# A planned attention and GeGLU block on one core: x1's statistics move from ScalarE to VectorE, the ones columns of V are set in four pieces, and the planner paces more zero fills

## The chip, the cores and the metric

The kernel runs on 1 core of one Trainium2 chip. The metric is device microseconds of one execution. A second, profiled execution gives the trace that is read here; its own time is given beside its span.

## The reference

One pre-norm transformer block without a mask, S = 2048 rows, D = 512, 32 heads of 16, F = 1792, all tensors bfloat16:

```python
x  = A_x                                             # (1, 2048, 512)
q, k, v = split_heads(layernorm(x) @ A_wqkv)         # 32 heads of 16
p  = softmax((q @ k.T) * 16 ** -0.5)                 # 2048 x 2048 for each head
h  = x + merge_heads(p @ v) @ A_wo
h2 = h + (gelu(layernorm(h) @ B_w_gate) * (layernorm(h) @ B_w_up)) @ B_w_down
```

`layernorm` is (x - mean) / sqrt(var + 1e-5) without weights, `gelu` is the tanh form.

## The kernel before

**Who decides the order.** The kernel is written as streams of operations (`Op`, one engine each, with a duration that the author expects). `Sched.run` plays these streams against its own clock when the kernel is built, picks the operation that can start first, breaks near ties by priority (`prio`, plus a random part of up to 0.3 from `self.rng`), and so writes one fixed instruction list for each engine. On the chip every engine works through its list in order and waits only for semaphores of what it reads or overwrites. A `gate` (such as `C["exp"] >= 1`) and an expected duration (such as the megabytes of a load) shape the list and leave no wait on the chip. Every change of a number in the planner therefore can move instructions anywhere in the kernel.

**The start.** x comes as 16 tiles of 128 rows in chunks of four: x0 in two loads, x1, x2, x3 in one load each, between them the pieces of the weights (`loads`). `ln1(c)` makes the statistics of a chunk: VectorE's `bn_stats` and `bn_aggr`; `ln1_rstd` makes 1/sqrt(var + eps) on GpSimd (a power); `ln1_norm` writes the normalised tile, on VectorE for chunks 0 and 1, on GpSimd for chunks 2 and 3. `ln1_T` turns the tile: for chunks 0 and 1 by four TensorE transposes and a copy from PSUM (ScalarE for tile 1, VectorE for the others, lines L1452 and L1454), for chunks 2 and 3 by a DMA transpose on SyncE's queue (L1437). Tile 4, the first of x1, has its statistics from ScalarE (lines L1388 and L1390: a sum and a sum of squares, then five small GpSimd operations, L1392 to L1400). `first()` projects K and Q of the first four heads tile by tile; `proj_kq` and `proj_v` do the rest, by need. `ones_v` sets the ones column behind every head of V (L1369), with which the product P·V also gives the softmax's denominator. `warm()` keeps TensorE busy with matmuls of no use until the first scores.

**The long middle.** A step of scores (`qk`) writes two PSUM banks, and ScalarE takes one `exp` of 128x1024 from them (`exps`, L1335). There are two pairs of banks, so the scores of a step wait for the exp two steps earlier. A part of the score tiles (124 groups of four) goes to VectorE instead, which makes their exponentials by integer arithmetic (`dconv` L1705, `dchain` L1718 to L1725, one of the four multiplications on GpSimd). `pv` and `group_pv` multiply by V. Query rows are done in chunks of 512, 512, 256, 256, 256, 128 and 128 (`CHUNKS`); while the next chunk's exps run, `post`, `gates`, `gelu`, `ups` and `downs` of the chunk before are woven in. A chunk's gelu is two ScalarE instructions (one for 128 rows) between two loads of ScalarE's function table (L1984 and back to exp at L1335). The last chunk's gelu goes straight from PSUM (L1967), after the exps have ended.

**Zero fills.** `fill()` lets the planner insert a matmul of zeros (L2051) when TensorE has done less than `RATE` columns per us over its last work. The debt `owed` grows with `RATE`; a fill goes into a gap of 0.217 us or more at a debt of 100, into a smaller gap at 300, into none at 800 (`OWED`). A fill is not inserted where, by the planner's clock, it would delay the scores that are due.

```python
if n < OWED[0] or (gap < TMM and n < OWED[1]) or (gap < 0.06 and n < OWED[2]):
    return False
```

Of the kernel before, what the change touches and what calls it, by code (L numbers as in the profile page):

```python
# [169 lines left out]
S, D, H, DH, F = 2048, 512, 32, 16, 1792  # L170
# [5 lines left out]
S, D, H, DH, F = 2048, 512, 32, 16, 1792  # L176
# [712 lines left out]
class Sched:  # L889
# [5 lines left out]
    def __init__(self, P, banks):  # L895
        self.P = P
        self.t = {n: 0.0 for n in P.ENGINES}
        self.done = {}
        self.streams = []
        self.banks = [(0.0, b) for b in banks]  # L900
        self.now = 0.0
        self.fill = None
        self.debt = (0.0, 0.0)
        self.pipe = 0.0
        self.lent = set()
        self.rng = random.Random(11)
        self.early = True
        self.wake = None
        self.port = 0.0
        self.room = lambda: False  # L910
        self.mode = "f"
        self.rows = [0.0] * 4
        self.due = self.INF
# [224 lines left out]
DB = 1  # L1138
HB = 0
CHP = -2.1  # L1140
RATE = 950
OWED = (100, 300, 800)
CHUNKS = (512, 512, 256, 256, 256, 128, 128)
F16, U16 = mybir.dt.float16, mybir.dt.uint16
# [60 lines left out]
def fast_path(nc, P, base0, ARENA, pbank, flag, A_x, A_wqkv, A_wo, B_x, B_w_gate, B_w_up, B_w_down, out):  # L1205
# [17 lines left out]
    VA = VF[:, 0:NVA].rearrange("p (t h i) -> p t h i", h=H, i=17)  # L1223
# [7 lines left out]
    x_sb = at("x_sb", [128, NT, D], BF16)  # L1231
# [106 lines left out]
    def loads():  # L1338
        def d(o, i, key, writes, mb):
            return Op("sp", mb, lambda e: e.dma_start(out=o, in_=i), writes=writes, dma=key)  # L1340
        def w(key, a, b, mb):
            return d(wqkv_sb[:, :, a:b], wv[:, :, a:b], key, [key], mb)
        def xl(c):
            return d(x_sb[:, 4 * c:4 * c + 4, :], xv[:, 4 * c:4 * c + 4, :], ("x", c), [("x", c)], 0.5)
        yield d(x_sb[:, 0:2, :], xv[:, 0:2, :], ("x", 0, 0), [("x", 0, 0)], 0.25)
        yield d(x_sb[:, 2:4, :], xv[:, 2:4, :], ("x", 0, 1), [("x", 0, 1)], 0.25)
        yield w("wk0", 512, 640, 0.18)
        yield w("wq0", 0, 128, 0.18)
        yield xl(1)
        yield w("wB", 640, 1536, 0.95)  # L1350
        yield xl(2)
        yield w("wA", 128, 512, 0.42)
        yield xl(3)
        yield d(wo_sb[:], A_wo.rearrange("(c p) j -> p c j", p=128), "wo", ["wo"], 0.5)
# [11 lines left out]
        yield Op("pool", 0.3, lambda e: e.tensor_copy(out=ident32[:], in_=ident[:]), reads=["ident"], writes=["ident32"])  # L1366

    def ones_v():
        yield Op("pool", 2.3, lambda e: e.memset(VA[:, :, :, 16:17], 1.0), writes=["VA_ones"], gate=lambda: ("xnT", 3) in C)  # L1369
        yield Op("pool", 0.1, lambda e: e.memset(VF[:, NVA:NVA + 15], 0.0), writes=["VA_ones"])  # L1370

    def masks():
# [8 lines left out]

    def ln1(c):
        ts_ = range(4 * c, 4 * c + 4)
        sa = ts_[0:1] if c == 1 else ()
        if sa:
            sl = slice(sa[0], sa[-1] + 1)
            for t in sa:
                yield Op("act", 0.52, lambda e, t=t: e.activation(out=sqj[:], in_=x_sb[:, t, :], func=ACT.Copy, accum_out=hsum[:, t:t + 1]),  # L1388
                         reads=[xkey(c, t)], writes=["sqj", ("hsum", t)])
                yield Op("act", 0.52, lambda e, t=t: e.activation(out=sqj[:], in_=x_sb[:, t, :], func=ACT.Square, accum_out=hsq[:, t:t + 1]),  # L1390
                         reads=[xkey(c, t)], writes=["sqj", ("hsq", t)])
            yield Op("pool", 0.3, lambda e: e.tensor_scalar(out=mv[:, sl, 0], in0=hsum[:, sl], scalar1=1.0 / D, scalar2=None, op0=ALU.mult),  # L1392
                     reads=[("hsum", t) for t in sa], writes=[("mv", t) for t in sa])
            yield Op("pool", 0.2, lambda e: e.tensor_tensor(out=htmp[:, sl], in0=mv[:, sl, 0], in1=mv[:, sl, 0], op=ALU.mult),
                     reads=[("mv", t) for t in sa], writes=["htmp"])
            yield Op("pool", 0.25, lambda e: e.tensor_scalar(out=rstd[:, sl], in0=hsq[:, sl], scalar1=1.0 / D, scalar2=EPS, op0=ALU.mult, op1=ALU.add),
                     reads=[("hsq", t) for t in sa], writes=[("rstd", t) for t in sa])
            yield Op("pool", 0.2, lambda e: e.tensor_tensor(out=rstd[:, sl], in0=rstd[:, sl], in1=htmp[:, sl], op=ALU.subtract),
                     reads=[("rstd", t) for t in sa] + ["htmp"], writes=[("rstd", t) for t in sa])
            yield Op("pool", 0.75, lambda e: e.tensor_tensor(out=rstd[:, sl], in0=rstd[:, sl], in1=nhalf[:, sl], op=ALU.pow),  # L1400
                     reads=[("rstd", t) for t in sa] + ["nhalf"], writes=[("rstd", t) for t in sa])
        for t in ts_:
            if t not in sa:
                yield Op("dve", 0.605, lambda e, t=t: e.bn_stats(out=stats[:, t, :], in_=x_sb[:, t, :]), reads=[xkey(c, t)], writes=[("stats", t)])
                yield Op("dve", 0.1, lambda e, t=t: e.bn_aggr(out=mv[:, t, :], in_=stats[:, t, :]), reads=[("stats", t)], writes=[("mv", t)])
                if c == 0:
                    yield Op("dve", 0.1, lambda e, t=t: e.tensor_scalar(out=rstd[:, t:t + 1], in0=mv[:, t, 1:2], scalar1=EPS, scalar2=None, op0=ALU.add), reads=[("mv", t)], writes=[("rstd0", t)])
                sch.add(ln1_rstd(t), 2 + 7 * c if c else -7.5)
            sch.add(ln1_norm(c, t), 2 + 7 * c if c else -7.5)
# [29 lines left out]
    def ln1_T(c, t):  # L1439
        if c >= TURN_X:  # L1440
            yield turn(xnT[:, t, :, :], xn_sb[:, t % 8, :], ("xT", t % 8), [("xn", t % 8)], [("xnT", t)])
            C[("xnT", t)] = 1
            C["ln1"] += 1
            return
        b = yield Acquire(reads=[("xn", t % 8), "ident"])
        pt = pbank[:, b, :].bitcast(BF16)
        yield Op("pe", 4 * TTR, cols=512, fns=[lambda e, dc=dc: e.transpose(out=pt[:, 128 * dc:128 * dc + 128], in_=xn_sb[:, t % 8, 128 * dc:128 * dc + 128], identity=ident[:])
                             for dc in range(4)], reads=[("xn", t % 8), "ident"], writes=[("pb", b)])
        C[("xnT", t)] = 1
        o_ap, i_ap = xnT[:, t, :, :], pt[:, 0:512].rearrange("p (c s) -> p c s", c=4)  # L1450
        if t in (1,):
            yield Op("act", 0.55, lambda e: e.activation(out=o_ap, in_=i_ap, func=ACT.Copy), reads=[("pb", b)], writes=[("xnT", t)])  # L1452
        else:
            yield Op("dve", 0.333, lambda e: e.tensor_copy(out=o_ap, in_=i_ap), reads=[("pb", b)], writes=[("xnT", t)])  # L1454
        sch.release(b)
        C["ln1"] += 1
# [13 lines left out]
    def first():  # L1470

        bq, bk = {}, {}
        for t in range(4):
            hf, o = t // 2, 128 * (t % 2)
            for nm, base, bank in (("wk0", D, bk), ("wq0", 0, bq)):
                if t % 2 == 0:
                    bank[hf] = yield Acquire(reads=[nm, ("xnT", t)])
                yield Op("pe", 4 * 0.062, cols=512, fns=[MM(pbank[:, bank[hf], o:o + 128], wqkv_sb[:, dc, base:base + 128], xnT[:, t, dc, :], dc == 0, dc == 3) for dc in range(4)],
# [661 lines left out]
```

## Time and profile before

| what | value |
|---|---|
| time before, median of 4 runs | 820.89 us (819.56 to 824.0) |
| the profiled execution's own time | 819.87 us |
| its span, first to last instruction | 818.0 us |
| around the span | 1.87 us |
| mean granted TensorE clock | 0.998 |
| TensorE (PE) busy | 767.4 us, 94% of the span |
| VectorE (DVE) busy | 759.8 us, 93% |
| ScalarE (ACT) busy | 769.7 us, 94% |
| GpSimd (POOL) busy | 252.5 us, 31% |
| the 776 exps of 128x1024 on ScalarE | 722.4 us |
| zero fills (L2051) in the trace | 105 matmuls, 36.7 us (135 weight loads) |

Busy shares are means over the whole span. Matmuls are pipelined and their ends are modelled, so a TensorE that is busy 94% is not at its peak. Idle time of an engine that does not set the pace costs nothing. A few matmul records are missing from the trace: 105 fills are recorded, 135 of their weight loads.

### The profile page before, as it was taken

Reading aid. Unit: us, or ns where it says so; the run is one execution under the profiler, and the core shown is the slowest. Engines: PE = TensorE matmul, PEld = TensorE weight load, DVE = VectorE, ACT = ScalarE, POOL = GpSimd, SP = SyncE. Lnnn points to the kernel's source line nnn. Section 1 sums busy time; section 2 is a strip of 40 time slices with the busy share of each in tenths; the row PEclk is TensorE's granted clock in tenths of the full one; section 3 lists DMA queues with packets and bytes.
Section 4 is the critical chain, followed back from the end, with each engine's and each line's share of the span. In section 5 each row is a group of like instructions: output and inputs, shape, how many; then the busy total and the mean of one; then the engine's idle time right before and its main releaser. Section 6 shows DMA issues by size and latency. Waiting matters only on the chain.

```text
span 818.0 us, 20122 instructions
## 1 busy us (share of the span) xinstructions
PE 767.4 (94%) x8194; PEld 274.3 (34%) x8261; DVE 759.8 (93%) x1238; ACT 769.7 (94%) x813; POOL 252.5 (31%) x305
## 2 busy tenths in 40 slices
PE   7999999989998999999999999999998999889996
PEld 3222222222222222222233333334433443345564
DVE  7679999999999999999999999999999999999964
ACT  3899999999999999999999999999999999999981
POOL 5703345632332322122133221222222212332310
PEclk9999999999999999999999999999999999999999
DMA  6200000350011000010111100110011000010100
GB/s 206 52 8 1 7 8 7 111 186 8 14 40 33 9 8 1 8 27 20 34 28 26 27 2 20 27 28 15 7 28 28 21 8 18 19 28 15 23 15 18
DMA packets 49878, 24.33 MB, mean 30 GB/s; under 512 B 39280, under 2 KB 48752, under 8 KB 49776
## 3 DMA queue, kind: packets, MB, share of 16 engines
q1 hardware_dynamic: 49776, 22.95, 10.7%
q8 instruction: 67, 1.10, 0.6%
q14 instruction: 35, 0.29, 0.1%
HBM read 11.80 MB, written 2.10 MB: 17 GB/s over the span
## 4 chain that ended last, share of the span: by engine, by line
PE 38%; DVE 28%; ACT 18%; issue 7%; DMA 3%; POOL 1%; ACTq 0%; DVEq 0%; POOLq 0%
PE pbank L1329 25%; ACT PT L1335 15%; PE pbank L1328 12%; DVE dXE L1705 12%; DVE dXE L1720 5%; DVE dXE L1718 4%; DVE dXE L1725 3%; DMA OAT<-OA 2%; ACT GUT L1984 1%; DVE OA L1809 1%; ACT L1335 1%; DVE GUT L1999 1%; POOL dXE L1722 1%; DVE GUT L1971 1%; ACT L1984 1%
## 5 line engine op out<-in xcount | busy, mean ns | idle before, releaser
L1335 ACT ACTIVATE PT<-pbank 128x1024 bf16<-128x1024 f32 x776 | 722.4, 1075 | 14.6 <-PE pbank L1329 12.1
L1329 PE MATMUL pbank<-QT,KT 32*128 32x512 bf16 (+1 forms) x2304 | 347.9, 359 | 27.1 <-ACT PT L1335 19.0
L1705 DVE TENSOR_SCALAR dXE<-pbank 128x512 uint16<-128x512 f32 x496 | 326.0, 680 | 10.5 <-PE pbank L1329 8.7
L1722 POOL TENSOR_TENSOR dXE<-dXE 128x512 f16<-128x512 f16 x124 | 155.8, 1257 | 357.2 <-DVE dXE L1720 357.2
L1329 PEld LDWEIGHTS pbank<-QT,KT 32*128 32x128 bf16 x2304 | 91.1, 91 | 299.1 <-ACT PT L1335 208.5
L1329 PE MATMUL pbank<-PT,VA 128*32 128x256 bf16 (+2 forms) x2704 | 130.3, 292 | 0.6 <-DVE dXE L1705 0.2
L1720 DVE TENSOR_TENSOR dXE<-dXE 128x1536 f16<-128x1536 f16 x124 | 123.2, 994 | 1.2
L1725 DVE TENSOR_SCALAR dXE<-dXE 128x2048 uint16<-128x2048 uint16 x124 | 87.7, 710 | 5.2 <-POOL dXE L1722 3.6
L1718 DVE TENSOR_SCALAR dXE<-dXE 128x2048 uint16<-128x2048 uint16 x124 | 89.3, 720 | 0.1
L1329 PE MATMUL pbank<-dXE,VA 128*32 128x256 f16 (+2 forms) x1760 | 76.4, 289 | 0.7 <-DVE dXE L1725 0.5
L1328 PE MATMUL pbank<-hnT_c,wg_sb 128*128 128x256 bf16 (+2 forms) x392 | 70.3, 291 | 1.9 <-DMA hnT_c<-OnT 1.0
L1329 PEld LDWEIGHTS pbank<-PT,VA 128*32 128x32 bf16 x2704 | 47.7, 96 | 60.8 <-issue 58.5
L1831 POOL TENSOR_TENSOR Otok<-OAT,LINV 128x128 bf16<-128x128 bf16 (+2 forms) x52 | 28.3, 561 | 108.1 <-DVE LINV L1825 105.0
L1328 PE MATMUL pbank<-hnT_c,wu_sb 128*128 128x256 bf16 (+2 forms) x392 | 59.1, 289 | 2.4 <-DVE GUT L1999 1.6
L1328 PE MATMUL pbank<-wd_sb,GUT 128*128 128x512 bf16 x200 | 54.2, 381 | 3.7 <-issue 3.7
L1329 PEld LDWEIGHTS pbank<-dXE,VA 128*32 128x32 bf16 x1760 | 31.6, 96 | 30.1 <-issue 17.3
L1999 DVE TENSOR_TENSOR GUT<-pbank,GUT 128x512 bf16<-128x512 f32 (+1 forms) x57 | 36.9, 670 | 4.3 <-PE pbank L1328 3.2
L1328 PE MATMUL pbank<-xnT,wqkv_sb 128*128 128x512 bf16 (+1 forms) x152 | 38.4, 349 | 1.6 <-DMA xnT<-xn_sb 1.0
L2051 PE MATMUL pbank<-ones_bf,zero_bf 128*128 128x512 bf16 x105 | 36.7, 386 | 1.3 <-issue 1.3
L1328 PEld LDWEIGHTS pbank<-hnT_c,wu_sb 128*128 128x128 bf16 x392 | 29.8, 98 | 23.6 <-issue 9.5
L1971 DVE CAST GUT<-pbank 128x512 bf16<-128x512 f32 (+1 forms) x53 | 35.8, 675 | 2.0 <-PE pbank L1328 1.9
L1328 PEld LDWEIGHTS pbank<-hnT_c,wg_sb 128*128 128x128 bf16 x392 | 24.9, 97 | 30.9 <-issue 27.2
(89 smaller groups left out, 345.7 us busy)
## 6 DMA issues: line engine op xcount, KB each, us to landing
xres<-in_A_x_dram SPq DMA_DIRECT2D x16, 128.0 KB, 2.2
out_dram<-out_sb SPq DMA_DIRECT2D x16, 128.0 KB, 1.7
wg_sb<-in_B_w_gate_dram SPq DMA_DIRECT2D x1, 1792.0 KB, 7.2
wu_sb<-in_B_w_up_dram SPq DMA_DIRECT2D x1, 1792.0 KB, 11.2
wd_sb<-in_B_w_down_dram SPq DMA_DIRECT2D x1, 1792.0 KB, 16.3
x_sb<-in_A_x_dram SPq DMA_DIRECT2D x3, 512.0 KB, 8.3
wqkv_sb<-in_A_wqkv_dram SPq DMA_DIRECT2D x1, 896.0 KB, 7.4
x_sb<-in_A_x_dram SPq DMA_DIRECT2D x2, 256.0 KB, 3.2
```

The lines of the kernel that those rows point to most:

```text
L1328: return lambda e: e.matmul(o, l, r, start=start, stop=stop)
L1329: return lambda e: e.matmul(o, l, r, start=start, stop=stop, tile_position=tile)
L1335: return lambda e: e.activation(out=o, in_=i, func=func, **kw)
L1705: yield Op("dve", 0.603, lambda e: e.tensor_scalar(out=dXE[G["k"] % NX][:, 0, j, :], in0=pbank[:, b, :], scalar1=XMIN + 1024.0 * CENTER, s ...
L1718: yield Op("dve", 0.07 + 0.133 * n, lambda e: e.tensor_scalar(out=W, in0=X, scalar1=0x3ff, scalar2=0xb800, op0=ALU.bitwise_and, op1=ALU.bi ...
L1720: yield Op("dve", 0.066 + 0.267 * nd, lambda e: e.tensor_tensor(out=W[:, 0:nd, :].bitcast(F16), in0=W[:, 0:nd, :].bitcast(F16), in1=X[:, 0 ...
L1722: yield Op("pool", TPOOL, lambda e, j=j: e.tensor_tensor(out=W[:, j, :].bitcast(F16), in0=W[:, j, :].bitcast(F16), in1=X[:, j, :].bitcast( ...
L1725: yield Op("dve", 0.07 + 0.133 * (h1 - h0), lambda e, h0=h0, h1=h1: e.tensor_scalar(out=X[:, h0:h1, :], in0=X[:, h0:h1, :], scalar1=0x7c00 ...
L1831: yield Op("pool" if turned else "dve", 0.15 + 0.55 / len(slots) if turned else 0.06 + 0.28 / len(slots), lambda e, o4=o4, lx=lx, o_ap=o_a ...
L1971: yield Op("dve", 0.07 + 0.001042 * n * CHUNKS[c], lambda e: e.tensor_copy(out=o_ap, in_=i_ap), reads=[("pb", b)], writes=keys, extra=dE)
L1999: yield Op("dve", 0.07 + 0.001042 * n * CHUNKS[c], lambda e: e.tensor_tensor(out=o_ap, in0=u_ap, in1=o_ap, op=ALU.mult), reads=[("pb", b)] ...
L2051: return Op("pe", TMM, lambda e: e.matmul(pbank[:, b, :], zero_bf[:], ones_bf[:], start=False, stop=False, skip_group_check=True), reads=[ ...
```

## The change

Seven edits, all in the planner's input. (1) The random seed goes from 11 to 9. (2) `RATE` goes from 950 to 1000 columns per us. (3) The planner expects other sizes of four loads (wk0, wq0, x1, wB); what is loaded, and in which order, stays. (4) The ones column of V is set by four GpSimd memsets of four tiles each in place of one of sixteen, planned after the first exp and marked as users of the port that GpSimd and VectorE share. (5) Tile 4 of x has its statistics from VectorE like all others: two ScalarE passes and five small GpSimd operations go, one `bn_stats`, one `bn_aggr` and two small GpSimd operations (an add and a power) come. (6) The copies of turned tiles 0 and 2 go from VectorE to ScalarE, beside that of tile 1. (7) For tiles 2 and 3 the first projection makes Q before K.

```diff
-        self.rng = random.Random(11)
+        self.rng = random.Random(9)
...
-RATE = 950
+RATE = 1000
...
-        yield w("wk0", 512, 640, 0.18)
-        yield w("wq0", 0, 128, 0.18)
-        yield xl(1)
-        yield w("wB", 640, 1536, 0.95)
+        yield w("wk0", 512, 640, 0.3)
+        yield w("wq0", 0, 128, 0.3)
+        yield d(x_sb[:, 4:8, :], xv[:, 4:8, :], ("x", 1), [("x", 1)], 0.9)
+        yield w("wB", 640, 1536, 0.35)
...
     def ones_v():
-        yield Op("pool", 2.3, lambda e: e.memset(VA[:, :, :, 16:17], 1.0), writes=["VA_ones"], gate=lambda: ("xnT", 3) in C)
+        for q in range(4):
+            yield Op("pool", 0.6, lambda e, q=q: e.memset(VA[:, 4 * q:4 * q + 4, :, 16:17], 1.0), writes=["VA_ones"], gate=lambda: C["exp"] >= 1, port=True)
...
-        sa = ts_[0:1] if c == 1 else ()
+        sa = ts_[0:0] if c == 1 else ()
...
-        if t in (1,):
+        if t in (0, 1, 2):
             yield Op("act", 0.55, lambda e: e.activation(out=o_ap, in_=i_ap, func=ACT.Copy), reads=[("pb", b)], writes=[("xnT", t)])
...
-            for nm, base, bank in (("wk0", D, bk), ("wq0", 0, bq)):
+            for nm, base, bank in (("wk0", D, bk), ("wq0", 0, bq))[::-1 if t > 1 else 1]:
```

The instruction lists of the two built kernels differ along their whole length. In number they differ little: both have 776 exps on ScalarE and 124 groups on VectorE. Zero fills go from 135 to 203. Around the gelus ScalarE loads its function table ten times in place of twelve: the gelu of the 128-row chunk before the last, which stood one exp before the end of the exps, now stands after the last exp. Four matmuls of P·V fewer come out of the other assignment of tiles to ScalarE and VectorE.

## The prediction

> **What bounds the kernel now.** I read the page first, then ScalarE's timeline, then the timelines of GpSimd, VectorE and TensorE where ScalarE stands still. The engine table shows three engines within 10 us of each other, so shares decide nothing:
>
> ```profile
> PE 767.4 (94%) x8194; PEld 274.3 (34%) x8261; DVE 759.8 (93%) x1238; ACT 769.7 (94%) x813; POOL 252.5 (31%) x305
> ```
>
> ScalarE's timeline (start, length, engine, line, tile, then idle time before and what ended it), in the first 110 us:
>
> ```profile
> 15.42 0.47 ACT L1490 ACTIVATE QT<-pbank,qmask 128x256 bf16<-128x256 f32 x1 [4.24 <-PE pbank L1328]
> 16.61 7.44 ACT L1335 ACTIVATE PT<-pbank 128x1024 bf16<-128x1024 f32 x8 [0.71 <-PE pbank L1329]
> 27.62 7.44 ACT L1335 ACTIVATE PT<-pbank 128x1024 bf16<-128x1024 f32 x8 [3.57 <-PE pbank L1329]
> 35.43 7.55 ACT L1335 ACTIVATE PT<-pbank 128x1024 bf16<-128x1024 f32 x8 [0.38 <-PE pbank L1329]
> 44.89 41.67 ACT L1335 ACTIVATE PT<-pbank 128x1024 bf16<-128x1024 f32 x44 [1.90 <-PE pbank L1329]
> ```
>
> Eight exps for each chunk of keys, and a stall before each batch of eight, until that chunk's K is there. From exp 25 at 44.89 on ScalarE hardly stops: the windows view gives it 733.41 us of work in the 741.65 us from there to the last scores (786.54), so 8.2 us idle. I split the span at these two points: 44.9 us of start, 741.7 us in which ScalarE sets the pace, 31.5 us of end.
>
> Who sets 44.89? The chain of waits around it:
>
> ```profile
> 38.05 0.78 POOL xn_sb L1432
> 38.84 3.55 DMA xnT<-xn_sb
> 42.64 1.02 PE pbank L1328 x4
> ```
>
> GpSimd normalises tile 15 until 38.82, the tile is turned by DMA, K is projected, and 6.07 us after GpSimd's end exp 25 runs. GpSimd's timeline is without a gap from tile 8's rstd at 19.74 to there: 19.1 us for 8 tiles, 2.4 us each. So the start is GpSimd's, not that of the first exp.
>
> The first exp itself hangs on a memset. GpSimd, VectorE, TensorE in the timeline:
>
> ```profile
> 10.93 2.46 DVE L1424 TENSOR_SCALAR xn_sb<-x_sb,mv,rstd 128x512 bf16<-128x512 bf16 x1
> ...
> 10.98 2.27 POOL L1369 MEMSET VA<- 128x512 bf16 x1
> ...
> 13.45 0.40 PE L1447 MATMUL pbank<-ident,xn_sb 128*128 128x128 bf16 x4 [1.70 <-DVE xn_sb L1424]
> ```
>
> The same VectorE operation took 0.38 to 0.41 us for tiles 0 to 2; beside the memset it took 2.46, and TensorE waited for it.
>
> **The change part by part.**
>
> *Ones column in four pieces.* Same elements: 4 x 0.57 = 2.27 us on GpSimd, plus about 0.1 for each of three handoffs within the engine (0.08 to 0.1 between dependent GpSimd rows). The gate on the first exp is the planner's only: in the new list the first memset follows tile 5's power and waits for nothing. I place that by VectorE's new order (tile 5's aggregate behind tile 4's normalisation, at 12.9) at 13.9 to 16.5. Tile 3's normalisation then costs 0.4 us in place of 2.46: 2.05 off the path of the first exp. What pays is GpSimd's queue: the memsets now stand in front of the rstds of tiles 6 and 7, and all of chunks 2 and 3.
>
> A rule bears on this. *The Trainium skill, "SBUF — State Buffer", section "Who interferes with whom", says that GpSimd and VectorE's two-port modes take one shared port pair as an exclusive lock, and whoever is first keeps it for its whole instruction; by that tile 3's normalisation, first by 0.05 us in the trace, should not have waited; the first exp would then gain 0.5 in place of 2.5, and the sum, which rests on exp 25, would stay.* I go by the row, 2.46 against 0.4: starts in the trace are not grants.
>
> *Tile 4's statistics.* ScalarE loses 0.63 + 0.63 + 0.19 + 0.19 = 1.4 us (7.81 to 9.3), which held the copy of tile 1 (transposed by 8.4, copied at 9.19). VectorE gets 0.68 + 0.18, GpSimd loses five rows (0.25 + 0.19 + 0.19 + 0.19 + 0.56 = 1.38) and gets 0.22 + 0.57: 0.6 less. *Copies of tiles 0 and 2 on ScalarE*: 0.58 each where ScalarE idles, 0.42 each off VectorE. *Q before K* for two tiles: four matmuls of 0.055, about 0.2 us earlier for the last Q.
>
> *First exp.* By the new lists: wB lands at 10.9 as now, and two V matmuls that wait for it stand ahead of tile 3's transpose. Then transpose 11.4, VectorE's copy 11.8 to 12.2, Q of tile 3 from 12.45, ScalarE's Q copy 12.9, against 15.42. The exp follows 1.19 later: 14.1, 2.5 us sooner. Almost none of it survives. Ten V matmuls (2.2 us at 0.218) now stand between the scores of exp 1 and exp 2, which puts exp 2 at 16.5 to 17.5, against 17.5 now. Exp 9 needs the copies of tiles 5 to 7, which VectorE's new list puts behind four V copies (0.6 each, to 22.7); tiles 5 to 7 copied at 24.5, four K matmuls, a K copy behind four other VectorE rows to 27.3, and 0.5 to the exp: 27.8, against 27.62.
>
> *Exp 25, by GpSimd's new list.* Tile 5's rstd from 13.0 (0.94), memsets 2.65, rstds of tiles 6 and 7 1.9: 18.5. Eight tiles at 2.4, less some 0.1 where two rows in a row do not depend on each other: 37.6, against 38.82. So exp 25 comes 1.2 us sooner, at 43.7, if what follows still takes 6.07. Bounds: ScalarE itself needs from exp 17 (35.2 at best) 7.5 us for eight exps, so 42.7, a gain of 2.2; if VectorE's queue makes tile 8's statistics late by as much as GpSimd's gaps show today (1.29 us before tile 8), nothing. I take 1.2, from the row sums.
>
> *The middle.* The same exps and five chunks' gelus with their table loads stand before the last scores, so ScalarE's work there is the same 733 us. What can move is its 8.2 us of waiting, by the new seed, the other place of every piece, and 68 more fills. A fill costs TensorE 0.218 us (four 512-column matmuls start 0.87 us before what follows), 14.8 us for 68. The windows of the fills alone:
>
> ```profile
> 200.00:300.00 100.00, 13.22 (x38) 3.44 (x45) 1.00 0.09 21
> 300.00:400.00 100.00, 1.94 (x5) 0.69 (x8) 1.00 0.06 14
> ```
>
> With 45 fills (weight loads) in the first window and 8 in the second, ScalarE idled 0.23 us in the first and 0.66 in the second. Fills in gaps cost nothing. In the new list 31 of the 68 more stand ahead of score tile 600 of 2048 (at some 230 us), 7 from there to tile 1000, and 20 from tile 1000 to 1200 (some 390 to 460 us), where 26 stand today. There TensorE idles 5.0 us in the 100 us from 400 on by the windows view, about 3.5 in these 70, and 20 fills take 4.4. So the price lies between nothing and 14.8 us, nearest to the row of the first window: nothing. They also bring nothing here, as the granted clock is 1.00 in each window up to 787. *The Trainium skill, "TensorE: Matmul & The Clock Gate", section "What's actually happening", lets the clock drop only after an idle window of some 3.4 us, which speaks against more fills; by it, too, they bring nothing.* The new order by itself can take from the 8.2 us or add as much; without a row that says which, zero.
>
> *The end.* Today the exp before the last is done at 787.30, and the last waits for a gelu between two table loads:
>
> ```profile
> 787.33 1.28 ACT L1984 ACT_TABLE_LOAD   x1
> 788.62 1.70 ACT L1984 ACTIVATE GUT<-GUT 128x1792 bf16<-128x1792 bf16 x1
> 790.33 1.28 ACT L1335 ACT_TABLE_LOAD   x1
> 791.63 1.02 ACT L1335 ACTIVATE PT<-pbank 128x1024 bf16<-128x1024 f32 x1
> ```
>
> After, the last exp ends 4.3 us sooner. But TensorE was not idle meanwhile: it did 23 matmuls of the down projection (4.91 us), and from the last scores to its last matmul (812.1) it works for all but some 1.5 of 25.5 us. The new list puts behind the last scores 24 gate matmuls of 128 columns more (1.34 us), 32 of P·V more (0.7), three down matmuls fewer (0.65): 25.4 if it never waits. So the 4.3 us turn into TensorE's queue: a gain of 0.1 to 0.7, I take 0.3; 1.5 lost if the chain from last exp to last normalised tile (9.7 us) is held up.
>
> **Sum.** -1.2 (start) + 0 (middle) - 0.3 (end) = -1.5 us. The profiled execution took 819.87, so 818.4; the median stands 1.0 above it, so 819.4.
>
> **The rivals.**
>
> *A, the forecast*: ScalarE-bound as before, 1.5 us off; own range 817 to 823. For it: the exp count is the same and fills were free where they are densest.
>
> *B, the new order closes ScalarE's waits.* 14 waits for scores make 5.5 us after 50 us, the longest 0.94, at places where two-bank scores come late behind other TensorE work. If the new order halves the 8.2 us, 4.1 go, and with the start's upper end of 2.2 and the 0.3 the time is 820.89 - 6.6 = 814.3. Against it: nothing in the edits aims there.
>
> *C, the fills get onto the path (slower).* The planner's clock is not the chip's: a fill planned into a gap that is not there delays the scores by 0.218, and ScalarE with them, since two bank pairs leave one exp of slack. Half of the 68 cost 7.4: 820.9 + 7.4 - 1.5 = 826.8. It decides from 26 fills on (5.7 us, as 1.5 are gained and 4.1 are 0.5%). For it: in the 100 us from 400 on TensorE's idle time is no longer than what the new fills ask for. Against it: the first window above.
>
> *D, the edits of the start don't do what they say*: the memset meets a normalisation again (tiles 5 and 6, when they come 1.5 us sooner than I place them), or the chunk-1 copies hold exp 9 by a us or two more. Then the start gives nothing or loses 1: 820.6 to 821.6, inside A's range.
>
> **How the numbers follow.** 0.5% is 4.1 us, about what a measurement can tell from no change: faster is below 816.8, slower above 825.0. A with D has 0.46, B 0.34, C 0.20. The range runs from 813.0 (a little below B's 814.3, as its lower bound with all of the 8.2 us gone is 810) to 825.5 (C's point of decision, with most of C left out).
>
> **What would show it.** Right: first exp at 14 to 14.5; normalisations of 0.4 us and none of 2; exp 25 at 43 to 44.5; ScalarE's idle time from there to the last scores at 6 to 10 us; last exp within 2 us of the last scores, and 31 us from the last scores to the end of the span. Wrong: exp 25 not before 44.9, then GpSimd's queue was not the bound or the memsets stood in it worse than priced; ScalarE's waits for scores above 13 us, with zero fills as the instructions ahead of the late scores, is C; below 5 is B.

## The result, and the profile after

The changed kernel takes 818.6 us (median of 34 runs, 816.5 to 828.8); the kernel before took 820.9 beside it (55 runs). The ratio is 0.9973 [0.9959, 0.9987], a gain of 2.2 us: real, but within the 0.5% that were called "no change". The profiled execution took 818.25 us with a span of 816.4, against 819.87 and 818.0. The forecast was 819.4 with a sum of -1.5 us; the two profiled executions differ by 1.6. The sum fits, but by luck, not by the terms it was made of (an exp is ScalarE's 128x1024 activation; exp 25 is the first on the last quarter of the keys):

| stretch (profiled execution) | before | after | difference | forecast |
|---|---|---|---|---|
| start of span to exp 25 | 44.89 | 44.93 | +0.04 | -1.2 |
| exp 25 to last scores | 741.65 | 740.23 | -1.42 | 0 |
| last scores to end of span | 31.46 | 31.24 | -0.22 | -0.3 |

The engine table of the page, and the group of zero fills, as before with their share of records missing (203 weight loads, 163 matmuls):

```profile
PE 778.0 (95%) x8247; PEld 277.5 (34%) x8325; DVE 758.8 (93%) x1238; ACT 766.4 (94%) x809; POOL 252.2 (31%) x305
...
L2052 PE MATMUL pbank<-ones_bf,zero_bf 128*128 128x512 bf16 x163 | 55.2, 388 | 2.1 <-issue 2.1
```

**The start.** ScalarE's timeline of the changed kernel (start, length, engine, line, then idle time before and its releaser):

```profile
14.47 1.02 ACT L1335 ACTIVATE PT<-pbank 128x1024 bf16<-128x1024 f32 x1 [0.73 <-PE pbank L1329]
17.06 6.52 ACT L1335 ACTIVATE PT<-pbank 128x1024 bf16<-128x1024 f32 x7 [1.56 <-PE pbank L1329]
29.15 7.44 ACT L1335 ACTIVATE PT<-pbank 128x1024 bf16<-128x1024 f32 x8 [5.57 <-PE pbank L1329]
36.96 7.55 ACT L1335 ACTIVATE PT<-pbank 128x1024 bf16<-128x1024 f32 x8 [0.37 <-PE pbank L1329]
44.93 35.70 ACT L1335 ACTIVATE PT<-pbank 128x1024 bf16<-128x1024 f32 x38 [0.42 <-PE pbank L1329]
```

Exp 1 is 2.1 us sooner (14.47), exp 9 is 1.5 us *later* (29.15, before 27.62), and exp 25 stands where it stood. The steps before that came out as worked out: the memsets lie at 14.30 and take 2.75 us, no normalisation is held, and GpSimd ends at 37.82 (forecast 37.6, before 38.82). Tile 3's normalisation and GpSimd's memsets and last row:

```profile
9.63 0.40 DVE L1425 TENSOR_SCALAR xn_sb<-x_sb,mv,rstd 128x512 bf16<-128x512 bf16 x1
```
```profile
14.30 2.75 POOL L1370 MEMSET VA<- 128x128 bf16 x4
...
37.05 0.77 POOL L1433 TENSOR_SCALAR xn_sb<-x_sb,rstd,htmp 128x512 bf16<-128x512 bf16 x1
```

GpSimd's us was not used, because exps 9 to 24 now run back to back behind a late exp 9. The windows view shows where exp 9 is lost (the stretch and its length in us, then busy us of TensorE, weight load, VectorE, ScalarE, GpSimd; then the granted clock, DMA share and GB/s). The first two lines are of the kernel before:

```profile
20.00:22.00 2.00, 1.89 (x20) 0.69 (x20) 1.83 (x6) 2.00 (x3) 1.61 (x4) 1.00 0.00 0
22.00:24.00 2.00, 1.28 (x10) 0.48 (x10) 2.00 (x6) 2.00 (x3) 1.56 (x6) 1.00 0.27 63
```
```profile
18.00:20.00 2.00, 0.81 (x6) 0.22 (x6) 1.95 (x7) 2.00 (x4) 1.32 (x5) 1.00 0.01 4
20.00:22.00 2.00, 1.34 (x14) 0.33 (x14) 1.97 (x5) 2.00 (x3) 1.83 (x5) 1.00 0.00 0
22.00:24.00 2.00, 2.00 (x16) 1.17 (x13) 1.58 (x4) 1.58 (x2) 1.57 (x6) 0.52 0.00 0
24.00:26.00 2.00, 2.00 (x15) 0.71 (x14) 1.89 (x5) 0.00 (x0) 1.73 (x5) 0.62 0.29 66
```

The V matmuls that used to lie here are done already, so TensorE has little to do from 18 to 22 us. From 22.1 to 25.5 us, 3.4 us long, it gets half its clock, in the very stretch in which it works without a pause for tiles 5 to 7. The profiled execution of the kernel before has no such drop in its start (that of experiment 12, with the same lists up to the tail, has one at 11.3 us).

**The middle.** From exp 25 to the last scores ScalarE has the same 733 us of work and waits 7.15 us in place of 8.24; its work is 0.33 shorter (before, then after):

```profile
44.89:786.54 741.65, 704.78 (x7652) 243.74 (x7707) 714.66 (x1134) 733.41 (x771) 225.71 (x236) 1.00 0.10 25
44.93:785.16 740.23, 713.52 (x7649) 244.13 (x7718) 714.43 (x1132) 733.08 (x771) 226.00 (x236) 1.00 0.10 25
```

**The end.** The last exp is done at 786.85 (before 792.65), with no gelu ahead of it; from there to the end of the span it is 29.55 us in place of 25.35. ScalarE's last rows:

```profile
769.00 17.84 ACT L1335 ACTIVATE PT<-pbank 128x1024 bf16<-128x1024 f32 x19
786.86 1.28 ACT L2027 ACT_TABLE_LOAD   x1
788.15 0.20 ACT L2027 ACTIVATE gset<-mv 128x1 f32<-128x1 f32 x1
795.88 1.70 ACT L1985 ACTIVATE GUT<-GUT 128x1792 bf16<-128x1792 bf16 x1 [7.53 <-DVE GUT L1972]
```

### The profile page after: what moved, and what is told of

It is laid out like the page before. It is cut to its first block, busy times and chain, and to the rows that moved or that the text cites. A ratio compares the mean times of both kernels' runs of the same rounds, so it can differ in the third digit from the quotient of the medians.

```text
span 816.4 us, 20261 instructions
## 1 busy us (share of the span) xinstructions
PE 778.0 (95%) x8247; PEld 277.5 (34%) x8325; DVE 758.8 (93%) x1238; ACT 766.4 (94%) x809; POOL 252.2 (31%) x305
## 4 chain that ended last, share of the span: by engine, by line
PE 38%; DVE 35%; ACT 16%; issue 7%; DMA 2%; POOL 1%; SPq 0%; DVEq 0%; ACTq 0%; POOLq 0%
PE pbank L1329 23%; DVE dXE L1706 15%; PE pbank L1328 14%; ACT PT L1335 13%; DVE dXE L1721 6%; DVE dXE L1719 5%; DVE dXE L1726 4%; DVE GUT L1972 1%; ACT GUT L1985 1%; DMA wqkv_sb<-in_A_wqkv_dram 1%; PE pbank L2052 1%; DVE OA L1810 1%; DMA OAT<-OA 1%; ACT L1335 1%; POOL dXE L1723 1%
## 5 line engine op out<-in xcount | busy, mean ns | idle before, releaser
L1335 ACT ACTIVATE PT<-pbank 128x1024 bf16<-128x1024 f32 x776 | 722.1, 1080 | 15.6 <-PE pbank L1329 13.3
L1723 POOL TENSOR_TENSOR dXE<-dXE 128x512 f16<-128x512 f16 x124 | 157.5, 1271 | 374.4 <-DVE dXE L1721 374.4
L1329 PEld LDWEIGHTS pbank<-QT,KT 32*128 32x128 bf16 x2304 | 89.2, 91 | 290.0 <-ACT PT L1335 202.7
L1726 DVE TENSOR_SCALAR dXE<-dXE 128x2048 uint16<-128x2048 uint16 x124 | 87.8, 711 | 4.8 <-POOL dXE L1723 3.5
L1719 DVE TENSOR_SCALAR dXE<-dXE 128x2048 uint16<-128x2048 uint16 x124 | 92.0, 742 | 0.1
L2052 PE MATMUL pbank<-ones_bf,zero_bf 128*128 128x512 bf16 x163 | 55.2, 388 | 2.1 <-issue 2.1
```

Source lines behind the costliest of these rows:

```text
L1329: return lambda e: e.matmul(o, l, r, start=start, stop=stop, tile_position=tile)
L1335: return lambda e: e.activation(out=o, in_=i, func=func, **kw)
L1719: yield Op("dve", 0.07 + 0.133 * n, lambda e: e.tensor_scalar(out=W, in0=X, scalar1=0x3ff, scalar2=0xb800, op0=ALU.bitwise_and, op1=ALU.bi ...
L1723: yield Op("pool", TPOOL, lambda e, j=j: e.tensor_tensor(out=W[:, j, :].bitcast(F16), in0=W[:, j, :].bitcast(F16), in1=X[:, j, :].bitcast( ...
L1726: yield Op("dve", 0.07 + 0.133 * (h1 - h0), lambda e, h0=h0, h1=h1: e.tensor_scalar(out=X[:, h0:h1, :], in0=X[:, h0:h1, :], scalar1=0x7c00 ...
L2052: return Op("pe", TMM, lambda e: e.matmul(pbank[:, b, :], zero_bf[:], ones_bf[:], start=False, stop=False, skip_group_check=True), reads=[ ...
```

## The experiments

Ratios are to the kernel before, run beside the experiments on the same chip; in the three groups of runs its median was 821.7 (1, 2, 5, 9), 822.6 (3, 6, 10, 11) and 822.0 us (4, 7, 8, 12). Where the clock of single runs is named, it is the mean granted TensorE clock that every run has beside its time. A trace comes from one run of each, and in experiments 1, 3, 5, 6 and 12 that was the slowest of its group. The instruction lists of experiments 5 to 11 are those of the changed kernel, but for what the edit itself adds.

**1. The start's edits alone** (the changed kernel with the old seed and `RATE`).

```diff
-        self.rng = random.Random(9)
+        self.rng = random.Random(11)
-RATE = 1000
+RATE = 950
```

> The changed kernel with the old seed 11 and the old RATE 950, so the edits of the start alone. Theory 1, the edits of the start move the first exp and not exp 25, and the gain comes from the middle's new order: exp 1 at 14 to 14.5, exp 25 at 44 to 45, 820 to 821.5, no difference from before that can be told. Rival, the edits of the start carry the gain: exp 25 at 43.5 or sooner, 818 to 819.

822.1 us (12 runs), ratio 0.9998 [0.9974, 1.0023]. Here the start does all that was forecast and more: exp 1 at 13.87, exp 9 at 26.36, exp 25 at 42.53, 2.4 us sooner than before, with the clock at 1.00. Nothing of it arrives: this plan has 780 exps on ScalarE, ScalarE waits 12.7 us from exp 25 to its last exp (8.3 before), and three drops of the clock (at 200, 316 and 504 us, 20.5 us in all) lie in the profiled execution. The drops are not the whole reason: its three runs at a clock of 0.999 took 819.6, 819.6 and 820.6, no less than the kernel before at 0.998 or more (819.3, the median of 20 runs).

**2. Seed and `RATE` alone** (the kernel before with seed 9 and `RATE` 1000).

> The kernel before with seed 9 and RATE 1000 and none of the other edits. Theory 1, seed and rate carry the gain by another order of the middle: ScalarE's idle time between exp 25 and the last scores near 7 us, 818.5 to 819.5. Rival, the edits of the start carry it: 820.5 to 821.5. A third reading, the middle is a draw that each new list makes again: anywhere from 816 to 825, with ScalarE's idle time from exp 25 to the last scores moving with the time.

830.4 us (6 runs), ratio 1.0111 [1.0064, 1.0157]. 780 exps again, 12.6 us of ScalarE's waiting, exp 25 at 45.93.

**3. The changed kernel with the old seed**, `RATE` 1000.

> The changed kernel with the old seed 11 (RATE 1000 and the edits of the start stay). Its planner gives ScalarE 778 exps instead of 776 and 230 fills. Theory 1, the seed is a draw of a plan, priced by what ScalarE must do and by the clock: 2 exps more are 1.9 us, exp 25 at 42.5 as with the edits of the start alone is 2.4 us less, few clock drops: 817 to 819.5. Rival, seed 9 is what makes the kernel fast: 821 or more.

828.1 us (4 runs), ratio 1.0069 [1.0027, 1.0111]: 778 exps, 14.9 us of waiting, although exp 25 starts at 43.69. Two drops of the clock (402 and 713 us, 13.7 us in all) lie in this trace.

**4. The changed kernel with the old `RATE`**, seed 9.

> The changed kernel with RATE back at 950; seed 9 and all edits of the start stay. This is the fourth corner beside seed 11 with 950, seed 11 with 1000 and the changed kernel. The new list has 784 exps on ScalarE in place of 776. Theory that the count of exps and ScalarE's waits, both drawn anew by any number of the planner, make the time: 8 exps at 0.93 are 7.4 us on the engine that sets the pace, so 824 to 828, ratio 1.004 to 1.008, whatever the fills do. Rival, that RATE 1000 pays through its fills: the clock is lower by 0.003 to 0.01 than in the changed kernel, and the time at an equal clock is that of the changed kernel plus at most 1. Second rival, that the edits of the start are what pays: ratio 0.997 as in the changed kernel.

822.5 us (12 runs), ratio 1.000 [0.997, 1.003]. The median is below the 824 to 828 of the first expectation and above the changed kernel (3.9 us by the medians, 2.2 by the ratios), which neither rival allows: at a mean clock of 0.995 its seven runs take 821.8 to 823.4 us, the changed kernel's seven 818.4 to 819.7. The eight exps more cost something, but less than 7.4 us. The page's group of exps and the window from exp 25 to the last scores:

```profile
L1335 ACT ACTIVATE PT<-pbank 128x1024 bf16<-128x1024 f32 x784 | 727.3, 1078 | 13.6 <-PE pbank L1329 11.5
```
```profile
44.80:788.21 743.41, 719.08 (x7691) 242.84 (x7690) 698.89 (x1105) 738.12 (x779) 224.89 (x232) 1.00 0.10 25
```

ScalarE's work rises by 5.0 us (738.12 against 733.08) and its waiting falls by 1.9 (5.29 against 7.15), since VectorE lost the groups that ScalarE took (698.89 us of work, 714.43 in the changed kernel). The stretch is 3.2 us longer, between the 2.2 and the 3.9.

The four corners with the new start, and the two with the old one:

| | `RATE` 950 | `RATE` 1000 |
|---|---|---|
| new start, seed 9 | 822.5 | **818.6** (the change) |
| new start, seed 11 | 822.1 | 828.1 |
| old start, seed 9 | not run | 830.4 |
| old start, seed 11 | **820.9** (before) | not run |

Six plans of one kernel cover 12 us, while the medians of before differ by less than 2 between groups. The change is the best of them; the kernel before and experiments 1 and 4 can't be told apart (ratios 0.9998 and 1.000). The two that were given are the only ones with 776 exps. No edit has an effect of its own that could be added: by the ratios, `RATE` 1000 gains 2.2 us with seed 9 and loses 5.8 with seed 11; seed 9 gains nothing that can be told at 950 and 7.9 at 1000.

**5. The clock of the start: scores of steps 3 to 8 issued twice**, in the changed kernel, to fill TensorE from 18 to 22 us with harmless work.

```diff
             fns, rd = scores(put)
+            if 2 <= st <= 7:
+                fns = fns + fns
```

> The changed kernel with the scores of steps 3 to 8 issued twice in a row (same result, 12 matmuls more, nothing else moved), where TensorE stood still between exps from 18 to 22 us and the granted clock then fell to 0.52 and 0.62 (22 to 26 us). Theory 1, the clock ate the start's gain: the clock stays at 0.95 or more in 22 to 26 us, exp 9 starts at 27.8 to 28.3 instead of 29.15, exp 25 at 43.7 to 44.1 instead of 44.93 (GpSimd's end 37.8 plus 6.07), and the time falls by about 1 us, to 817.6. Rival, VectorE's queue of V copies holds exp 9 whatever the clock: the clock is back but exp 9 stays at 29.0 to 29.3, exp 25 at 44.9, the time at 818.6.

817.9 us (12 runs), ratio 0.9945 [0.9921, 0.9969]. But the profiled execution does not support the reason: TensorE is busy for 2.47 of the 3.4 us before 21.9 us (in the changed kernel 1.86 of the 3.4 before 22.1), and yet the clock halves for two windows (21.9 to 28.7 us); exp 9 falls to 31.83 and exp 25 to 47.61, and its span is 819.2. Exp 1 is late too (15.38), as the weights wB were first used at 12.21.

**6. The same with zeros**: two full-width zero matmuls ahead of the scores of each of these steps.

```diff
+            if 2 <= st <= 7:
+                z = lambda e, b0=b0: e.matmul(pbank[:, b0, :], zero_bf[:], ones_bf[:], start=True, stop=True)
+                fns, rd = [z, z] + fns, rd + ["zero_bf", "ones_bf"]
```

> The changed kernel with two zero matmuls of full size put ahead of the scores of steps 3 to 8, in the bank that these scores then overwrite (12 in all; the lists of the other engines stay). Issuing the scores twice had left the clock drop in the trace: scores use 32 of the array's 128 rows. Theory 1, the clock drop at 22 to 26 us is what ate the start's gain, and full-size matmuls prevent it: granted clock 1.00 from 18 to 32 us, exp 9 at 27.6 to 28.3, exp 25 at 43.7 to 44.2, time 1 to 1.5 us under the changed kernel's, ratio to before 0.995 to 0.996. Rival, VectorE's V copies hold exp 9: clock 1.00 but exp 9 at 29 or later, and no difference from the changed kernel's 0.9973.

818.7 us (6 runs), ratio 0.9969 [0.9927, 1.0011]. The clock is 1.00 from 18 to 32 us, and exp 9 still comes at 29.36 and exp 25 at 45.15: the twelve zeros push TensorE's own queue, so that tile 5's transpose starts at 24.05 in place of 22.38. They cost what they save. (Its span of 825.6 comes from 20.5 us at half clock from 751 us on.)

**7. One zero in place of two.**

```diff
-                fns, rd = [z, z] + fns, rd + ["zero_bf", "ones_bf"]
+                fns, rd = [z] + fns, rd + ["zero_bf", "ones_bf"]
```

> The changed kernel with one full-width matmul of zeros (0.217 us) ahead of the scores of each of steps 3 to 8, in place of the two of the earlier run. If the granted clock falls in the start because TensorE is given too little full-width work between 18 and 22 us, and if the twelve zeros of the earlier run cost by their length what they saved, six keep the clock at 1.00 there for half the price: exp 9 at 28.4 (29.15 in the changed kernel, 29.36 with twelve), exp 25 at 44.2 (44.93), and 0.7 us off the changed kernel's time, ratio to before 0.996. Rival: six zeros do not keep the clock; the dip of one window stays, exp 9 stays at 29 to 30 and the time that of the changed kernel, ratio 0.997.

The mechanism holds in this profile, and both milestones come within 0.3 us of the number. Windows, then ScalarE:

```profile
18.00:20.00 2.00, 1.61 (x9) 0.38 (x6) 1.97 (x6) 1.79 (x3) 1.23 (x5) 1.00 0.02 4
20.00:22.00 2.00, 1.70 (x14) 0.50 (x14) 1.97 (x5) 2.00 (x4) 1.84 (x5) 1.00 0.00 0
22.00:24.00 2.00, 2.00 (x25) 1.06 (x17) 1.65 (x4) 1.81 (x2) 1.54 (x6) 1.00 0.00 0
```
```profile
28.15 7.44 ACT L1335 ACTIVATE PT<-pbank 128x1024 bf16<-128x1024 f32 x8 [4.18 <-PE pbank L1329]
35.96 7.55 ACT L1335 ACTIVATE PT<-pbank 128x1024 bf16<-128x1024 f32 x8 [0.38 <-PE pbank L1329]
43.93 16.06 ACT L1335 ACTIVATE PT<-pbank 128x1024 bf16<-128x1024 f32 x17 [0.42 <-PE pbank L1329]
```

With the clock held, exp 25 starts 0.96 us sooner than before, where the forecast had 1.2. The time does not follow: 819.0 us (12 runs), ratio 0.9974 [0.9946, 1.0002], as the changed kernel; the span is 816.2, and the middle is 1.0 us longer (741.22). The lists there are the changed kernel's, and the trace shows where the us goes: exp 351 still starts 1.02 us ahead of the changed kernel's (358.36 against 359.38). Then a reciprocal in VectorE's list waits for a DMA transpose, which landed after 4.3 us in place of 2.4; the scores behind it are late, and ScalarE stands still for a us. The reciprocal in the changed kernel, then here, and ScalarE here:

```profile
382.31 0.24 DVE L1826 RECIPROCAL LINV<-OAT 128x16 f32<-128x16 bf16 x1
```
```profile
382.74 0.25 DVE L1829 RECIPROCAL LINV<-OAT 128x16 f32<-128x16 bf16 x1 [1.37 <-DMA OAT<-OA]
384.67 3.84 ACT L1335 ACTIVATE PT<-pbank 128x1024 bf16<-128x1024 f32 x4 [1.00 <-PE pbank L1329]
```

Whether the unprofiled runs lose it at the same place is not known.

**8. The scores twice, once more.**

> The kernel with the scores of steps 3 to 8 issued twice once more, beside the others of this call. Theory that its first result is its own: 817.9, ratio 0.992 to 0.997, below the changed kernel's by 0.7. Rival, that it is the changed kernel's time within the spread of runs, since its profiled exp 25 came 2.7 us later: ratio 0.996 to 0.999.

818.0 us (12 runs), ratio 0.9955 [0.9922, 0.9988]. Of the same kernel as in 5, this profiled execution has *no* drop in its start, with the same 2.47 us of TensorE's work from 18.5 to 21.9; exp 25 is at 45.02. Here too the weights wB were late (12.22, before 10.94), and exp 1 came at 15.39, with experiment 5's 15.38. So the two profiled starts of one kernel are alike up to exp 1 and differ by 3.1 us at exp 9 and 2.6 at exp 25, with the clock as what sets them apart. Experiment 5, then this one:

```profile
15.38 1.02 ACT L1335 ACTIVATE PT<-pbank 128x1024 bf16<-128x1024 f32 x1 [0.73 <-PE pbank L1329]
31.83 7.44 ACT L1335 ACTIVATE PT<-pbank 128x1024 bf16<-128x1024 f32 x8 [6.07 <-PE pbank L1329]
22.00:24.00 2.00, 2.00 (x14) 0.27 (x12) 2.00 (x4) 1.68 (x2) 1.58 (x6) 0.50 0.00 0
```
```profile
15.39 1.02 ACT L1335 ACTIVATE PT<-pbank 128x1024 bf16<-128x1024 f32 x1 [0.73 <-PE pbank L1329]
28.73 7.44 ACT L1335 ACTIVATE PT<-pbank 128x1024 bf16<-128x1024 f32 x8 [4.18 <-PE pbank L1329]
22.00:24.00 2.00, 2.00 (x24) 0.70 (x21) 2.00 (x5) 2.00 (x3) 1.58 (x6) 1.00 0.00 0
```

What the start loses or gains is handed on nearly whole through the middle, as the traces of one order with no drop of the clock in the middle show (us against the changed kernel's trace):

| trace | exp 25 | exp 351 | end of span |
|---|---|---|---|
| experiment 7 | -1.0 | -1.0 | -0.2 |
| experiment 8 | +0.1 | 0.0 | -0.4 |
| experiment 11 | +1.65 | +1.64 | +1.3 |
| experiment 5 | +2.7 | +2.7 | +2.8 |

The largest shift behind exp 351 is that of the same DMA transpose: it landed after 2.4 us in the changed kernel and experiment 11, 3.3 in experiment 8, 3.6 in 5 and 4.3 in 7, and the exps behind it come 0, 0.4, 0.7 and 1.35 us later. In 10 of its 24 runs the mean clock is 0.998 or more, in 7 of 12 with one zero, in 3 of 36 of the changed kernel. That fits a drop in the start that has become rarer, not impossible; the mean clock does not say where a drop lies. The two medians of this kernel are the lowest of all that ran; their intervals overlap that of the changed kernel, so it is not shown to beat it.

**9. All zero fills thin**: the fills keep their places, with 32 columns in place of 512 (here and in `fill_op`).

```diff
-            op = Op("pe", TMM, lambda e: e.matmul(pbank[:, b, :], zero_bf[:], ones_bf[:], start=True, stop=True), reads=["zero_bf", "ones_bf"], writes=[("pb", b)], cols=390)
+            op = Op("pe", TMM, lambda e: e.matmul(pbank[:, b, 0:32], zero_bf[:], ones_bf[:, 0:32], start=True, stop=True), reads=["zero_bf", "ones_bf"], writes=[("pb", b)], cols=390)
```

> The changed kernel with every zero fill cut from 512 columns to 32 (same place, same semaphores, weight load kept), which takes some 200 ns of TensorE from each of 203. Theory 1, fills in gaps are free and bring nothing: 818.6 within 1 us, granted clock 1.00 in the windows from 50 to 787 us. Rival A, some fills delay scores: ScalarE's idle time from exp 25 to the last scores falls from 7.2 us by 1 to 3, and the time with it. Rival B, fills hold the clock up: the granted clock falls below 0.98 in windows with many fills (200 to 300 us, 390 to 460 us) and the time rises by 2 us or more.

864.0 us (6 runs, 846 to 879), mean clock 0.859 to 0.910. The page's row of the clock in 40 slices, and a window:

```profile
PEclk9899999586576999999668999999999999969999
```
```profile
197.00:243.00 46.00, 44.70 (x275) 10.47 (x277) 37.50 (x56) 38.81 (x41) 12.70 (x10) 0.52 0.08 18
```

Half clock comes in stretches of 3.4 to 44.4 us, multiples of about 3.4, and inside the longest TensorE is recorded as busy 97% of the time. From exp 25 to the last one ScalarE waits 28.3 us. From 50 us to the last scores the changed kernel's trace has none of them, with the same lists. So it is the fills that hold the clock there; the old kernel was not run without its 135.

**10. Every third fill thin** (137 full, 68 thin: about the number of full fills of before, in the changed kernel's lists).

```diff
+    nf = [0]
+
+    def cut():
+        nf[0] += 1
+        return 32 if nf[0] % 3 == 0 else 512
```

> The changed kernel with every third zero fill cut from 512 to 32 columns: 137 full fills are left of 205, as many as before, in the same lists. Theory 1, the added fills keep the clock up and that is the change's gain: runs with a mean clock under 0.994 become frequent again (a third or more of them; 3 of 36 with the changed kernel, 11 of 23 before), the median rises by 2 us or more, to 820.5 to 825. Rival, the gain is the new order of the middle: median 818 to 819.5 and clocks as with the changed kernel.

819.7 us (6 runs), ratio 0.9965 [0.9933, 0.9997]; the kernel of experiment 11, with the same lists and all fills full, had 819.7 in the same group. The clocks with thin fills are lower (0.990 to 0.995, there 0.995 to 0.999), the time is the same; the trace has one half-rate window in the middle (192 us), over which ScalarE's exps slip by 0.9 us. The thin third is not the added 68 themselves, so these are not shown to pay, nor shown to be of no use.

**11. One memset for the whole ones column**, at the place of the first of the four; the other three write one element each.

```diff
-e.memset(VA[:, 4 * q:4 * q + 4, :, 16:17], 1.0)
+e.memset(VA[:, 4 * q:4 * q + 1, 0:1, 16:17] if q else VA[:, :, :, 16:17], 1.0)
```

> The changed kernel with the first of the four memsets writing the whole ones column (and the other three one element each), so one long memset in the new place; all lists stay the same. Theory 1, the place did it and the split does nothing, as no VectorE normalisation stands beside the memsets: no VectorE row longer than 0.8 us from 14 to 18 us, exp 9 and exp 25 within 0.3 us of the changed kernel's 29.15 and 44.93, ratio 0.997. Rival, the split matters: a VectorE operation of 1.5 us or more beside the memset, exp 9 later by that.

819.7 us (6 runs), ratio 0.9957 [0.9925, 0.9989]. GpSimd and, from VectorE, tile 4's normalisation ahead of it and tiles 5 and 6 behind it:

```profile
14.73 2.76 POOL L1370 MEMSET VA<- 128x512 bf16 x4
```
```profile
13.33 0.40 DVE L1425 TENSOR_SCALAR xn_sb<-x_sb,mv,rstd 128x512 bf16<-128x512 bf16 x1
...
18.54 0.73 DVE L1425 TENSOR_SCALAR xn_sb<-x_sb,mv,rstd 128x512 bf16<-128x512 bf16 x2
```

2.28 us for the whole column (2.76 with the three small ones), 2.75 in four pieces, no normalisation held either way: in this order the place did it, and the split does nothing. That is not so in every order. With the old seed (experiment 1; in 3 alike) two normalisations of VectorE fall beside the pieces: the first takes 0.38 us and the second 0.81, against 2.46 beside the whole memset in the kernel before:

```profile
13.61 2.88 POOL L1370 MEMSET VA<- 128x128 bf16 x4
```
```profile
14.79 1.11 DVE L1425 TENSOR_SCALAR xn_sb<-x_sb,mv,rstd 128x512 bf16<-128x512 bf16 x2
```

So where they meet, a piece of 0.64 us costs a normalisation 0.4 us and the whole one cost it 2.1. In the changed order, the profiled start with one memset has a drop of two windows (21.1 to 27.9 us): exp 9 at 30.79, exp 25 at 46.58.

**12. The gelu alone**: the kernel before, with the gelu of the 128-row chunk held until the last exp; the lists are those of before up to the tail. The `Op` of `gelu` (L1984) gets one argument more.

```diff
+    gate=(lambda: "expdone" in C) if c == NC - 2 else None
```

> The kernel before with one edit: the gelu of the 128-row chunk before the last is held until the last exp. The instruction lists are those of before up to some 30 us from the end; only the tail's order changes, as in the changed kernel. The prediction's end term: the last exp ends 4.3 us sooner (about 788.4 in place of 792.65 in the trace), and the time falls by 0.1 to 0.7 us, because TensorE's queue from the last scores on is full; the distance from the last exp's end to the end of the span grows from 25.35 to about 29.4. Rival: the last exp is on the path, and the whole 4.3 us come off (ratio 0.995). Second rival: the gelu that now starts later holds the last down projections up, 1.5 us lost (ratio 1.002).

819.7 us (12 runs), ratio 0.998 [0.9949, 1.0011]; among runs with a clock of 0.998 and more the median is 818.35 (6 runs) against 819.3 (20 runs of before), 1.0 us less, where the runs of before alone spread from 816.9 to 821.0. The profiled execution lost its time elsewhere (27.3 us at half clock from 728 us on), but its tail can be read:

```profile
795.55 3.77 ACT L1335 ACTIVATE PT<-pbank 128x1024 bf16<-128x1024 f32 x4 [0.22 <-PE pbank L1329]
799.34 1.28 ACT L1984 ACT_TABLE_LOAD   x1
800.64 1.70 ACT L1984 ACTIVATE GUT<-GUT 128x1792 bf16<-128x1792 bf16 x1
```

From the last scores (797.64) to the end of the span (827.7) it is 30.06 us, 1.4 less than before; from the last exp's end (799.32) 28.38, 3.0 more. Of the 4.3 us, 3.0 turn into TensorE's queue and 1.4 come off this tail. The times agree (1.0), but are not clear of their spread. By the tail both rivals, all 4.3 and a loss of 1.5, fall.

## Why the prediction was right, and where it was not

**The time** was right within 0.8 us (819.4, measured 818.6), and it lies in A's own range. The sum of -1.5 stands beside -1.6 in the traces, through two errors that cancel: luck.

**The start, -1.2: the size of the gain on GpSimd was right, the step from there to exp 25 failed.** "Exp 25 comes 1.2 us sooner, if what follows still takes 6.07" took GpSimd's chain for the bound (6.07 became 7.11), and exp 9 at 27.8 was worked out with TensorE at full clock. In the changed kernel exp 9 is at 29.15; from there ScalarE itself needs 15.8 us for 16 exps, which is 44.93. By the prediction's own sign of being wrong ("exp 25 not before 44.9") the step is wrong, and it is rival D's outcome by a cause which D did not name.

The cause is the clock. Experiments 5 and 8, one kernel with exp 1 at the same time, have exp 9 3.1 us apart with two half-rate windows and none. The distance from exp 1 to exp 9, which leaves the landing of wB out, follows their number in all starts of seed 9 with the new edits: none 13.3 and 13.9 us (experiments 8 and 7), one 14.7 (three kernels), two 15.5 to 16.5 (experiments 9, 11 and 5). One does not fit, 14.7 without a drop: that start had the twelve zeros. The prediction's own distance was 13.7 (14.1 to 27.8). So of the 1.35 us that exp 9 lacks, some 0.4 are exp 1's and 0.8 to 1 the window's.

With the clock held (experiment 7) the term came to -0.96, about as worked out, but even there not by the wait that it names: exp 25 follows exp 9 by the same 15.8 us. And 6.07 is no fixed price: in experiment 1 exp 25 ran 4.9 us after GpSimd's end (37.61). A smaller slip moves nothing: ScalarE's four rows for tile 4 add up to 1.64, not 1.4.

**The middle, 0: off by 1.4 us, as far as one trace of each can tell.** Five traces of the changed kernel's order without a drop there have 739.9 to 741.2 us for this stretch, so a good part of the 1.4 can be the spread of executions. The prediction said that the new order could take from ScalarE's 8.2 us of waiting or add as much, and put zero for want of a row. The direction can't be read from a profile of before; experiments 1 to 4 show the size of the lottery: 5.3 to 14.9 us of waiting (in 1 and 3 partly under half clock), and 778 to 784 exps. Rival B named the mechanism, but about a quarter of what it asked for happened (1.1 of 4.1 us of waiting). Rival C (fills delay scores) is not seen: ScalarE's waiting fell with 68 fills more.

**"They also bring nothing here": wrong as an argument.** The clock of 1.00 in every window was taken as a sign that fills were not needed. Experiment 9 shows that it was their effect: without their columns the time rises by 45 us. For the 68 more the statement is neither shown nor refuted (experiment 10). The Trainium skill, "TensorE: Matmul & The Clock Gate", section "What's actually happening", has a free-running window of about 3.4 us and two states of the clock gate; the drops here agree with the length and the half rate (3.4 us, granted clock 0.5). The condition of its table for the low state, an idle window, does not fit these records: the clock halved after windows in which TensorE was recorded busy for 55% (the changed kernel) and 73% (experiment 5) of the time.

**The memset: right in its size, and the row was the right guide.** 0.40 us in place of 2.46 for tile 3's normalisation, and exp 1 at 14.47 (forecast 14.1; wB landed 0.4 later than assumed). The Trainium skill, "SBUF — State Buffer", section "Who interferes with whom", would have let the earlier starter keep the port, from which the prediction worked out a gain of 0.5 for exp 1 in place of 2.5; measured are 2.1, so the row decides.

**The end, -0.3: right in total, not in its parts.** -0.2 in the change; the gelu's move alone is worth 1.4 in the trace of experiment 12, above the 0.1 to 0.7 given for it, so the rest of the new tail gives back about a us. That part is a difference of two measurements and was not isolated.

**What stays open.** Why this plan and not its neighbours has 776 exps and little waiting was not followed into the planner, so the cause of the 2.2 us stays open. How much of them is the clock is not settled: at a mean clock of 0.996 the medians are 818.4 (15 runs after) and 821.25 (only 2 runs before), and the lines through all runs (last section) give 818.7 and 821.1 there, so about as much is left at an equal clock; in 29 of 69 runs of before the clock is under 0.994, in 3 of 36 after. That the new plan drops its clock less often is in these counts; that the fills are the reason is not shown.

## What to carry to other kernels

Where a planner draws the whole order anew from any number in its input, no edit has an effect of its own: run the corners (each edit with the old and with the new seed) before crediting one, and expect the plan's lottery, here 12 us, to be larger than what the edits were made for. A milestone that comes sooner counts only if the next wait behind it does not move: look which engine runs without a pause from there on, and at which clock. What ScalarE won or lost in the start here was still there 300 us later; one late DMA behind it could take it. A granted clock of 1.00 does not say that the work which holds it is free to go: take that work away once and look.

## What the runs showed of the hardware

- TensorE's granted clock falls to one half in whole stretches of 3.4 us (3.4, 6.8, 10.2, 13.7, 20.5, 27.3, 44.4 us were seen), after windows with 55 and 73% of recorded busy time in the start, and it stays low at 97% (experiment 9). Ahead of the drops in the start stand scores with 32 of 128 rows and few other matmuls. Experiments 5 and 8, one kernel with the same 73% before the place, had a drop and none; a share of 80% (experiment 7) had none.
- The time follows the mean granted clock of a run: a line through 69 runs of before gives 0.64 us for each 0.001, through 36 runs of the changed kernel 0.63. Runs of before lie between 0.971 (837.9 us) and 0.999 (819.6).
- The load wB was first used at 10.6 to 12.2 us in the profiled starts, where the clock was full up to there, of kernels that issue it alike, and moved exp 1 by as much (13.77 at 10.60, 15.39 at 12.22). One DMA transpose, at the same place of one list, landed after 2.4, 3.3, 3.6 and 4.3 us in four traces.
